# Moving two weight sums in the fifth unit, and block sums, sums of x and the turn of w in the sixth, of a linear-attention and SiLU kernel

## The chip, the cores and the metric

The kernel runs on one core of a Trainium2 chip. A core has five engines that each work through their own instructions in order: TensorE (PE, matrix products; its weight loads are shown apart as PEld), VectorE (DVE), ScalarE (ACT), GpSimd (POOL) and SyncE (SP), which here issues nearly all DMA transfers. They wait for each other through semaphores. SBUF is the on-chip memory of 128 partitions, PSUM holds the results of TensorE. The metric is the time of one execution on the device, in microseconds; lower is better.

## The reference, cut to what matters

First a linear attention with a decaying state (batch 4, 8 heads, 768 time steps, head size 48), then a two-layer block with SiLU on its output (3072 tokens, 384 to 2048 to 384), all in float32:

```python
for t in range(S):
    kt, vt, rt, wt = k[:, :, t], v[:, :, t], r[:, :, t], w[:, :, t]
    cur = einsum('bhd,bhe->bhde', u[None] * kt, vt)
    y[:, :, t] = einsum('bhd,bhde->bhe', rt, state + cur)
    state = wt[..., None] * state + einsum('bhd,bhe->bhde', kt, vt)
x = y.transpose(0, 2, 1, 3).reshape(B * S, H * D)
h = x @ w_in
out = (h / (1 + exp(-h))) @ w_out
```

## The kernel before, in words

The 768 steps are cut into 6 stretches of 128, and the batch into 2 pairs, which gives 12 **units** of 128 steps and two batch rows each. They are numbered from 0, so the fifth unit has `i == 4` (`NPAIR` is 4, `NFAST` is 3) and the sixth `i == 5`. The order of all instructions is written out by hand; there is no scheduler, and each engine follows its own part of the recorded order.

Inside a unit the 128 by 128 scores of a head are built in 7 levels. Level `l` takes blocks of `2 << l` steps: the later half's queries against the earlier half's keys. For that the decays `w` are turned so that time runs along the free dimension (`turn`, a transpose on VectorE, two per unit), and `product` (POOL, L414) multiplies neighbours, from 128 values to 64 and so on, into `tw1` to `tw7`. `grow_keys` (POOL, L646) multiplies the keys on to the next level, and `grow_queries` and `prepare` (VectorE, L628 and L783) the queries. `odd_keys` (ScalarE, L616) copies half of the keys to where the next level reads them. From the fourth unit on the products of two levels come in a `burst` (TensorE, L704): levels 3 and 4, then levels 5 and 6. `keep_level` puts them into `score`, by masked copies on VectorE (L722) for small levels and by copies on ScalarE (L804) for the levels 5 and 6.

The levels 0 to 2, the 8 by 8 blocks along the diagonal, are done another way from the fifth unit on. `block_bonus` (POOL, L497) makes products of queries and keys in token order, in steps 0 to 7, and `block_sum` (VectorE, L534) reduces them into `block_sums`: sum 0 and 1 after steps 1 and 2, sum 2 after step 4, sum 3 after step 6, sum 4 after step 7. Step 4 and step 7 write the same tile `ruk`, so sum 2 has to read it before step 7. `block_move(i, False)` then sends `block_sums` to DRAM (`kept`, L556), and `block_move(i, True)` brings it back in another layout in five transfers (`spare<-kept`, L561 and L563). The tokens of the next unit (`load_rk`, L158) go into tiles that step 7 reads last. `block_turn` (L567) shuffles one half of the block sums, and `block_write` (VectorE, L573) puts them into `score`, once for each half.

Beside a unit's attention runs the two-layer block of earlier units. In each call of `mix(i)` there is a list of groups with a count: the steps of a group are recorded, then so many steps of the block are recorded behind them. These are the seven quarter products of the second layer of unit `i - 2` (`quarter`, L1333, whose partial results are joined on VectorE in L1341 and on ScalarE in L1338) and then the twenty products of the first layer of unit `i - 1` (`first_layer`, L1189). The quarter products add into PSUM places that are used again: the seventh of them waits until VectorE has added the fifth to a known part (`ob`, L1341). The first layer from unit 3 on needs fewer products because sums of parts are formed first, of the weights once and for all (`in_weight_sum`, L1128, named `q1` to `q19`) and of x for every unit (`sums_of_x`, VectorE, steps 0 to 7, L1150 to L1170). Its products stand in the order

```python
ORDER = (20, 18, 14, 13, 2, 15, 4, 7, 19, 16, 1, 12, 9, 11, 3, 6, 10, 5, 8, 17)
```

(the keys alone), and VectorE joins their results in PSUM between them (`join`, L1216). Product 9 reads the weight sum `q9`; product 17 adds to a PSUM place that the join behind product 10 writes. The second burst stands between the products 11 and 3. At the end, `sums` (VectorE, L1304) makes eight differences of the SiLU results, which the quarter products of the next `mix` read from `temps`.

At the end of a unit `end[1]` records the state products, the scores by the values (L847 to L868), the turn of the next unit's keys (L365), two block sums, and the update. The next unit begins with the turn of its queries and `grow_own` (POOL, L655).

## Time and profile before

| what | us |
|---|---|
| median of three runs (568.08 to 572.91) | 568.59 |
| the profiled execution | 568.89 |
| its span, first to last instruction | 567.1 |
| TensorE busy in the span | 555.3 |
| VectorE busy | 477.7 |
| GpSimd busy | 395.4 |
| ScalarE busy | 275.1 |
| sixth unit (212.85 to 257.60): length, TensorE busy | 44.75, 43.17 |
| seventh unit (257.60 to 300.19) | 42.59, 42.59 |
| eighth unit (300.19 to 342.62) | 42.43, 42.43 |

The granted TensorE clock was 1.00 throughout. A line of a timeline has the start, the time taken, the engine, the source line, the operation and its tiles, the shape, and after `x` how many neighbours were merged into the line. In brackets stands how long the engine had been idle before, and which engine and line ended that. `SPq` is SyncE's issuing of a transfer, not the transfer. Matrix products overlap, so a product's time can be longer than its step in the sequence. `p_o`, `p_h`, `p_m`, `p_sc` are PSUM tiles, `tk`, `tr`, `tw` the turned keys, queries and decays.

### The profile page before, as it was taken

The page shows a single profiled execution, that of the slowest core. Times are in us where ns is not written, and L with a number is a line of the kernel's source. Part 1 is how long each engine was busy: PE and PEld are TensorE (multiplying, and loading weights), DVE is VectorE, ACT ScalarE, POOL GpSimd, SP SyncE. Part 2 cuts the span into 40 slices and gives each one's busy share as a digit, 9 for nine tenths or more (in the row PEclk, how much of TensorE's full clock was granted, in tenths as well). Part 3 has the DMA queues.
Part 4 walks back from the last instruction along what each step waited for, and adds up shares of the span by engine and source line. Part 5 has one row for each costly group of instructions (what it writes and reads, how often), then busy time and mean ns, then how long its engine had stood idle before and what let it go on. Part 6 is the DMA issues. An engine that isn't in the chain of part 4 may idle for free.

```text
span 567.1 us, 18885 instructions
## 1 busy us (share of the span) xinstructions
PE 555.3 (98%) x7782; PEld 517.6 (91%) x7782; DVE 477.7 (84%) x744; ACT 275.1 (49%) x620; POOL 395.4 (70%) x447
## 2 busy tenths in 40 slices
PE   8989999999999999999999999999999999999997
PEld 8767786699889989899999999999999999999997
DVE  6969788999999999899989989989989989882250
ACT  5679696362371373374274274274274272371330
POOL 5998998717879998797696696696696696700000
PEclk9999999999999999999999999999999999999999
DMA  9866967345445355365465454455555462102000
GB/s 204 266 139 185 241 210 143 48 60 118 107 73 102 77 109 93 60 130 94 101 103 93 104 100 90 106 96 93 108 92 96 91 108 65 38 5 57 29 9 21
DMA packets 206485, 57.59 MB, mean 102 GB/s; under 512 B 186048, under 2 KB 198208, under 8 KB 206400
## 3 DMA queue, kind: packets, MB, share of 16 engines
q1 hardware_dynamic: 203712, 54.23, 46.2%
q10 hardware_dynamic: 2688, 2.16, 1.5%
q8 instruction: 61, 1.00, 0.8%
q14 instruction: 24, 0.20, 0.1%
HBM read 47.14 MB, written 9.18 MB: 99 GB/s over the span
## 4 chain that ended last, share of the span: by engine, by line
PE 73%; POOL 10%; DVE 6%; SPq 5%; DMA 3%; issue 2%; ACT 0%; ACTq 0%; DVEq 0%; POOLq 0%
PE p_o L1333 23%; PE p_o L1189 14%; PE p_h L1189 9%; PE p_h L1082 7%; PE p_h L1333 4%; PE p_m L1271 4%; SPq L127 3%; PE p_sc L704 2%; PE p_m L868 2%; POOL tk L646 2%; DMA raw<-in_w_dram 2%; PE p_sc L1333 2%; PE p_m L847 1%; PE p_m L704 1%; DMA w_out_sb<-in_moe_w_in_dram 1%
## 5 line engine op out<-in xcount | busy, mean ns | idle before, releaser
L646 POOL TENSOR_TENSOR tk<-tk,tw 128x256 f32<-128x256 f32 x112 | 93.0, 851 | 7.9 <-DVE tw L414 3.8
L1333 PE MATMUL p_o<-own,temps 128*128 128x192 f32 x496 | 82.8, 326 | 0.0
L1333 PEld LDWEIGHTS p_o<-own,temps 128*128 128x128 f32 x496 | 80.8, 190 | 0.2 <-DVE temps L1304 0.2
L1189 PE MATMUL p_o<-xt,w_in_sb 128*64 128x128 f32 x1152 | 72.2, 273 | 0.8 <-POOL w_in_sb L1128 0.8
L414 POOL TENSOR_TENSOR tw<-tw 128x256 f32<-128x256 f32 (+6 forms) x71 | 40.5, 571 | 41.4 <-DVE tw L365 38.0
L1082 PE MATMUL p_h<-xt,w_in_sb 128*128 128x256 f32 x288 | 66.1, 384 | 1.8 <-POOL w_in_sb L260 1.6
L1189 PEld LDWEIGHTS p_o<-xt,w_in_sb 128*64 128x64 f32 x1152 | 64.6, 137 | 1.1 <-POOL w_in_sb L1128 1.1
L1082 PEld LDWEIGHTS p_h<-xt,w_in_sb 128*128 128x128 f32 x288 | 53.6, 190 | 10.0 <-POOL w_in_sb L260 2.4
L1333 PE MATMUL p_o<-w_out_sb,gt 128*128 128x192 f32 x308 | 54.5, 330 | 1.3 <-DVE ob L1341 1.3
L497 POOL TENSOR_TENSOR ruk<-tokens_rk 128x384 f32<-128x384 f32 x48 | 53.1, 1127 | 2.5 <-DMA tokens_rk<-in_k_dram 2.5
L628 DVE TENSOR_TENSOR tr<-tr,tw 128x512 f32<-128x512 f32 x57 | 51.9, 910 | 1.0 <-PE p_m L704 0.4
L1333 PEld LDWEIGHTS p_o<-w_out_sb,gt 128*128 128x128 f32 x308 | 50.0, 190 | 2.4 <-DVE ob L1341 1.6
L655 POOL TENSOR_TENSOR tk<-tk,tw 128x256 f32<-128x256 f32 x32 | 24.7, 800 | 31.6 <-DVE tk L365 31.6
L1304 DVE TENSOR_TENSOR temps<-gt 128x512 f32<-128x512 f32 (+1 forms) x48 | 43.1, 934 | 0.0
L1338 ACT COPY partial<-p_o 128x192 f32<-128x192 f32 x31 | 9.9, 319 | 67.5 <-PE p_o L1333 67.5
L1213 ACT ACTIVATE gt<-p_o 128x512 f32<-128x512 f32 x45 | 26.0, 601 | 25.7 <-PE p_o L1189 25.7
L616 ACT COPY tk<-tk 128x256 f32<-128x256 f32 x52 | 20.9, 402 | 33.7 <-POOL tk L646 25.0
L1333 PE MATMUL p_o<-w_out_sb,temps 128*128 128x192 f32 x176 | 30.4, 326 | 0.0
L722 DVE COPY_PREDICATED score<-mask,p_sc 128x512 f32<-128x512 int8 x38 | 28.4, 806 | 1.4 <-PE p_sc L704 1.3
L1333 PE MATMUL p_h<-w_out_sb,gt 128*128 128x192 f32 x168 | 29.1, 326 | 0.0
L497 POOL TENSOR_TENSOR spare<-tokens_rk 128x384 f32<-128x384 f32 x24 | 28.5, 1200 | 0.6
L1333 PEld LDWEIGHTS p_o<-w_out_sb,temps 128*128 128x128 f32 x176 | 28.9, 190 | 0.0
(251 smaller groups left out, 1316.7 us busy)
## 6 DMA issues: line engine op xcount, KB each, us to landing
w_out_sb<-in_moe_w_in_dram SPq DMA_DIRECT2D x6, 768.0 KB, 7.6
turned<-yt SPq DMA_DIRECT2D x18, 192.0 KB, 2.6
xt<-turned SPq DMA_DIRECT2D x9, 384.0 KB, 3.2
w_out_sb<-in_moe_w_out_dram SPq DMA_DIRECT2D x4, 768.0 KB, 5.2
own<-in_moe_w_out_dram SPq DMA_DIRECT2D x4, 768.0 KB, 5.7
tokens_w<-in_w_dram SPq DMA_DIRECT2D x8, 384.0 KB, 4.4
tokens_rk<-in_r_dram SPq DMA_DIRECT2D x7, 384.0 KB, 4.3
tokens_rk<-in_k_dram SPq DMA_DIRECT2D x7, 384.0 KB, 5.3
```

Source lines behind the costliest of these rows:

```text
L414: engine.tensor_tensor(out=up, in0=t[:, :, 0::2], in1=t[:, :, 1::2], op=ALU.mult)
L497: mul = lambda out, one, two: nc.gpsimd.tensor_tensor(out=out, in0=one, in1=two, op=ALU.mult)
L628: nc.vector.tensor_tensor(out=odd, in0=odd, in1=tw[i][l][:, :, 0::2][:, :, :, None].to_broadcast([128, Q, L >> (l + 1), c]), op=ALU.mult)
L646: nc.gpsimd.tensor_tensor(out=out, in0=have, in1=odd_products(i, l, b, *blocks), op=ALU.mult)
L655: nc.gpsimd.tensor_tensor(out=have, in0=have, in1=odd_products(i, l, b, [2, NP * ni]), op=ALU.mult)
L722: nc.vector.copy_predicated(out=dst, mask=masks[l][:, :, None].to_broadcast([128, NB, NP, ni, c]), data=sc[e].rearrange("p (b q) (i c) -> ...
L1082: nc.tensor.matmul(p_h[:, a, :], lhsT=w_in_sb[:, c, f * 128:(f + 1) * 128], rhs=xt[i][:, c, :], start=(a == 0 and c == 0), stop=(a == 1 an ...
L1189: nc.tensor.matmul(p[h:h + PD, q, :], lhsT=left[:, f:f + PD], rhs=right, start=first and q == 0, stop=q == 3, skip_group_check=True)
L1213: nc.scalar.activation(out=g(f, t), in_=have, func=AF.Silu)
L1271: nc.tensor.matmul(po[i, b], lhsT=gt[i, f // 2][:, f % 2, b * L:(b + 1) * L], rhs=w_out_sb[:, f, :], start=(f == 0), stop=(f == FC - 1))
L1304: nc.vector.tensor_tensor(out=out, in0=one, in1=two, op=op)
L1333: nc.tensor.matmul(p, lhsT=left(f), rhs=right[:, f, :], start=which in (0, 1, 3) and f == 0, stop=f == FH - 1, skip_group_check=True)
```

## The change

In the fifth unit the weight sums q5 and q9 are recorded one group earlier, ahead of `go_on(4, 4)`, which holds the key products of level 4. In the sixth unit (`tight`), sum 2 goes from ahead of `prepare(5, 3)` to behind step 3 of the sums of x, where step 7 of the bonus and steps 4 to 6 of the sums of x follow it, in a group of their own. Sum 4 and the sending of the block sums to DRAM go two groups later, behind the token loads of the next unit and the first four loads of its r, and right ahead of the transfers that bring them back. The two turns of the next w and its seven products, which stood around `keep_level(5, 4)` and `go_on(5, 4)`, go to the end of the unit, between the two block writes. No instruction is added or taken away.

```diff
+                tight = i == NPAIR + 1
-                keys_2 = [(odd_keys, i, 2), (grow_keys, i, 2, False), (grow_queries, i, 2), *sum_steps(i, 2)]
+                keys_2 = [(odd_keys, i, 2), (grow_keys, i, 2, False), (grow_queries, i, 2), *at(not tight, *sum_steps(i, 2))]
...
-                          ([*at(i in (NPAIR + 1, len(units) - 1), (sums_of_x, j, 0, 1)), (sums_of_x, j, 2), *bonus_steps(i, 6, 7), (sums_of_x, j, 3, 4, 5, 6), *loads("k", 3)], 2),
-                          ([(burst, i, 3), *at(i > NPAIR + 1, *sum_steps(i, 3)), (keep_level, i, 3), *at(i == NPAIR + 1, *sum_steps(i, 3)), *sum_steps(i, 4)], 2),
-                          ([(block_move, i, False), *at(ahead, (load_rk, i + 1, (0, 1))), *at(ahead and i > NPAIR + 1, (turn, i + 1, 0, "w"))], 1),
+                          ([*at(tight or i == len(units) - 1, (sums_of_x, j, 0, 1)), (sums_of_x, j, 2), *bonus_steps(i, 6), *at(not tight, *bonus_steps(i, 7)), (sums_of_x, j, 3), *at(not tight, (sums_of_x, j, 4, 5, 6)), *loads("k", 3)], 1 if tight else 2),
+                          *at(tight, ([*sum_steps(i, 2), *bonus_steps(i, 7), (sums_of_x, j, 4, 5, 6)], 1)),
+                          ([(burst, i, 3), *at(not tight, *sum_steps(i, 3)), (keep_level, i, 3), *sum_steps(i, 3 if tight else 4)], 2),
+                          ([*at(not tight, (block_move, i, False)), *at(ahead, (load_rk, i + 1, (0, 1))), *at(ahead and not tight, (turn, i + 1, 0, "w"))], 1),
                           ([*loads("r", 0)], 1),
-                          ([(block_move, i, True), *at(i == NPAIR + 1, (turn, i + 1, 0, "w")), *at(ahead, (turn, i + 1, 1, "w"), *products_of(i + 1, 0, 1, 2)), (keep_level, i, 4)], 2),
-                          ([(go_on, i, 4), *at(ahead, *products_of(i + 1, 3, 4, 5, 6))], 1),
+                          ([*at(tight, *sum_steps(i, 4), (block_move, i, False)), *at(not tight, (block_move, i, True)), *at(ahead and not tight, (turn, i + 1, 1, "w"), *products_of(i + 1, 0, 1, 2)), (keep_level, i, 4)], 2),
+                          ([*at(tight, (block_move, i, True)), (go_on, i, 4), *at(ahead and not tight, *products_of(i + 1, 3, 4, 5, 6))], 1),
...
-                          ([(keep_level, i, 5, 1), (keep_level, i, 6, 1)], 1),
+                          ([(keep_level, i, 5, 1), (keep_level, i, 6, 1), *at(tight, *both(turn, i + 1, "w"), *products_of(i + 1, *range(NL)))], 1),
...
-            for place, engine, names in ((0, nc.gpsimd, ("u1", "u", "q19")), (5, nc.gpsimd, ("q7",)), (8, nc.gpsimd, ("q8", "q1")),
-                                         (9, nc.gpsimd, ("q5", "q9")), (14, nc.gpsimd, ("q6", "q17"))):
+            for place, engine, names in ((0, nc.gpsimd, ("u1", "u", "q19")), (5, nc.gpsimd, ("q7",)), (8, nc.gpsimd, ("q8", "q1", "q5", "q9")),
+                                         (14, nc.gpsimd, ("q6", "q17"))):
```

## The prediction

> **What bounds the kernel.** I read the page first, then TensorE's waits, then the timelines of the fifth and sixth unit, engine by engine. All times below are on the clock of the profiled run of before.
>
> ```profile
> span 567.1 us, 18885 instructions
> PE 555.3 (98%) x7782; PEld 517.6 (91%) x7782; DVE 477.7 (84%) x744; ACT 275.1 (49%) x620; POOL 395.4 (70%) x447
> ```
>
> TensorE works in 555.3 of 567.1 us, and the change takes no matrix product away. So all it can win is idle time of TensorE in two of twelve units. The list of TensorE's waits says how much that is:
>
> ```profile
> PE p_o L1333 <- DVE ob L1341: 1.3, 1, 1.3
> PE p_o L1189 <- POOL w_in_sb L1128: 0.8, 1, 0.8
> PE p_m L704 <- POOL tk L646: 0.2, 1, 0.2
> ```
>
> Each happens once: the 0.83 us at 199.55 in the fifth unit, the 1.35 us at 228.72 and the 0.23 us at 247.3 in the sixth. The table of stretches, one per unit (sixth, then seventh), shows the room: length, then TensorE's busy time, then the other engines'.
>
> ```profile
> 212.85:257.60 44.75, 43.17 (x693) 41.69 (x689) 40.99 (x63) 20.40 (x52) 38.65 (x46) 1.00 0.50 92
> 257.60:300.19 42.59, 42.59 (x693) 41.58 (x689) 39.36 (x60) 20.58 (x52) 33.48 (x38) 1.00 0.53 99
> ```
>
> The sixth unit idles 1.58 us, the seventh not at all, but there VectorE (third figure, 39.36 of 42.59) is nearly as full as TensorE. That is where the bill for moved work would be sent. VectorE's timeline over the border of the two units:
>
> ```profile
> 227.86 1.13 DVE L534 TENSOR_REDUCE block_sums<-ruk 128x4 f32<-128x192 f32 x4 [0.89 <-POOL ruk L497]
> 229.66 0.36 DVE L1341 TENSOR_TENSOR ob<-p_o,partial 128x192 f32<-128x192 f32 x1
> ...
> 248.89 0.22 DVE L567 STREAM_SHUFFLE spare<-spare 128x64 f32<-128x64 f32 x1
> ...
> 261.27 1.30 DVE L365 STREAM_TRANSPOSE tk<-raw 128x512 f32<-128x512 f32 x2
> ...
> 272.88 0.36 DVE L1341 TENSOR_TENSOR ob<-p_o,partial 128x192 f32<-128x192 f32 x1
> ```
>
> From 248.26 to 280.2 the timeline shows no idle time of VectorE. The last line is the seventh unit's `ob` addition, for which TensorE's last quarter product (L1333) waits: it ends at 273.24 and that product starts at 273.30. So there is 0.06 us of slack, and whatever delays VectorE in that stretch delays TensorE by the same amount.
>
> **The change, part by part.**
>
> *Fifth unit, POOL.* Before, POOL runs the level-4 key products (196.02, 1.67 us), then q5 and q9 (197.65 and 199.00, to 200.34), then the level-5 key products (1.65, to 201.94). Now q5 and q9 come first and end at 198.7, so product 9 no longer waits: 0.83 us gone. The level-4 keys end at 200.35 and the level-5 keys at 202.0, as POOL's total is the same. The burst that needs them would start at 201.46 (202.29 less 0.83), its second half at 201.97: a tie. Nothing else on POOL moves. Of the 0.83, what goes on depends on VectorE, which carries the chain from there: ScalarE's silu for product 9 can move only from 201.53 to 201.25, its next copy from 202.41 to 201.75, so VectorE's next join from 203.03 to 202.4. I take **-0.6** (bounds 0 and -0.83).
>
> *Sixth unit, the 1.35 us.* The four reductions (1.13, after 0.89 waiting for POOL) leave the place ahead of L783 and `ob`. VectorE's query product ends at 226.96, L783 takes 0.72, `ob` then runs from 227.6 to 228.0, before TensorE is ready at 228.72. The reductions now stand behind the first sums of x, end near 232, and POOL's product that overwrites their input starts at 235.72: covered by 3.7 us. The two turns of w (1.2 us at 239.2) leave, sum 4 goes behind the next join, and the level-5 keys no longer stand behind w products. So the 0.23 goes too, and with 0.1 of slack in a join TensorE comes to the last part of the unit **1.67** us earlier. This gain lasts only if VectorE can follow.
>
> *Sixth unit, the block sums' way through DRAM.* SyncE's queue before:
>
> ```profile
> 238.71 0.33 SPq L556 DMA_DIRECT2D kept<-block_sums  x1
> 239.13 0.56 SPq L158 DMA_DIRECT2D tokens_rk<-in_r_dram  x1
> 239.74 0.59 SPq L158 DMA_DIRECT2D tokens_rk<-in_k_dram  x1
> 240.38 2.06 SPq L127 DMA_DIRECT2D raw<-in_r_dram  x4
> 242.54 0.41 SPq L561 DMA_DIRECT2D spare<-kept  x1
> 242.99 3.81 SPq L563 DMA_DIRECT2D spare<-kept  x4
> ```
>
> Now `kept` stands behind the two token loads (384 KB each) and four loads of r, with its return right behind it. The token loads wait for POOL's last product that reads the old tokens, which ends at 237.70 (235.72 and 1.98). So they issue at 237.8, and `kept` 3.4 us later (242.54 less 239.13), at 241.2. A transfer in that place took 4.1 us to land (the longest of the five `spare` transfers; the last took 1.8), so 245.3. In the fifth unit five issues straight after each other began over 2.5 us. The last is out at 247.9 and lands 1.8 later: **249.8** (bounds: 247.2, when VectorE wants it, and 251.3, if a write needs 1.4 more). Before, it was there at 248.2 and the shuffle ran at 248.89. The queue's later loads move back by 1.3 us and stay ahead of the yt copy that the following transfer awaits.
>
> [...]
>
> *End of the sixth unit.* Both turns of w (1.25 us) now stand behind the first block write, ahead of the join for product 17. With the shuffle at 249.8: block write 1.5, turns 1.25, join 0.65, together with the shuffle's 0.25 to 253.5. TensorE wants product 17 at 250.9 (252.53 less 1.67) and waits 2.6: it is 1.0 later than before. POOL gets seven w products (2.69 and 1.59 = 4.28 us) after the turns, and three bonus products (3.47, 1.44, 1.34) behind them, so it works until about 263.3, where before it was free from 258.27:
>
> ```profile
> 262.06 3.06 POOL L655 TENSOR_TENSOR tk<-tk,tw 128x256 f32<-128x256 f32 x4 [3.78 <-DVE tk L365]
> ```
>
> VectorE's eight subtractions (L1304) stand there. While POOL works one takes 1.48 us, while it rests 0.68; before they took 8.2 us in all, half of them slow. Starting at 255.4, I get five slow ones and three fast ones: 9.05, so 0.85 more (bounds 5.4 and 11.1 in all). [...]
>
> *The sum.* The seventh unit's `ob` moves by 249.8 - 248.9 = 0.9 for the shuffle, 1.25 for the turns and 0.85 for the subtractions: 3.0 later, and TensorE with it, since its slack was 0.06. The 1.67 is eaten inside these 3.0. With the fifth unit: 3.0 - 0.6 = **+2.4 us**. The profiled execution took 568.89 around its span of 567.1, so 571.3; the median of the runs is 568.59, 0.3 below that execution, so the sum may read high by that.
>
> **Rivals.**
>
> *The block sums are back in time.* If `kept` lands in 1.5 us, as the first one before did with nothing ahead of it, and its return is not held either, the shuffle runs when wanted, at 247.2. Then `ob` moves by -1.7 + 1.25 + 0.85 = 0.4, and the sum is -0.2: 568.7. For it: `kept` is a write, the loads ahead are reads of DRAM. Against it: the 4.1 us of `spare` in that very place. [...]
>
> *Faster: POOL leaves VectorE its pace.* POOL's idle time now lies between its last key product and the turns, and six of the seven w products are short (0.2 to 0.9 us). If the eight subtractions find it quiet, they take 5.4 instead of 8.2. The sum is then -0.6 + 0.9 + 1.25 - 2.8 = -1.3: 567.6. It decides from five fast subtractions of eight. Against it: the bonus products, 6.25 us of long operations, follow without a break.
>
> *Much slower.* If the block sums land after 253 us, the scores are late too, and the sum passes +5.7: 574.6 or more. Only the fifth unit's 5.5 us landings, taken twice, get there.
>
> *The edit does not do what it says.* If the burst waits for the later level-4 and level-5 keys, the 0.83 us only changes its name and the sum is +3.0: 571.9.
>
> **How the numbers follow.** The forecast (569.9 to 573.2, likeliest 571.3) gets 0.55, the block sums in time 0.20, the faster one 0.17, the empty edit 0.03, the much slower one 0.05. The range 567.0 to 573.4 takes in the second, most of the third, and the landing bounds (247.2 and 251.3 are -2.6 and +1.5 around 249.8). One per cent is 5.7 us, about what a measurement of this kernel can tell from no change; all cases but one lie inside: faster 0.01, same 0.95, slower 0.04.
>
> **What would show it.** In the profile after, the two waits of 0.8 and 1.3 us are gone from TensorE's list. In their place stands a wait of product 17, a `first_layer` product, for VectorE at the end of the sixth unit, about 2.6 us, and one of the last quarter product for `ob` in the seventh, about 2. The shuffle has an idle time ended by a DMA. If the shuffle follows without idle time, the DMA step is wrong; if the seventh unit's `ob` comes before TensorE wants it, the VectorE step is wrong. The prediction fails at the top if the late w products also hold the key products of the seventh unit, which had 5.3 us of cover (the level-3 keys end at 270.83, the burst starts at 276.09).

## The result and the profile after

The changed kernel takes 572.68 us (median of nine executions, 570.24 to 575.36) against 568.59 for the kernel before (568.08 to 572.91, also nine). The ratio is 1.0063, with a 95% interval of 1.0036 to 1.0091: a loss of about 0.6%, inside the one per cent that the prediction called no change. The ratio is taken over all the executions and is not the quotient of the medians, which would be 1.0072. A single execution is left out of a ratio as slow, one of 577.33 us of the kernel with the fifth unit's part alone, 1.7% above the fastest of that kernel. The profiled execution took 570.24 us around a span of 568.4; that of before took 568.89 around 567.1. So the profiled pair differs by 1.35 us and the medians by 4.1. Both figures need an explanation, and they have different ones. (The profiled execution of before lies 0.3 above its median, that of after 2.4 below.)

The changed kernel has two lines more around L1030, so all later line numbers shift by two: L1218 is the join of L1216, L1306 the differences of L1304, L1335 the quarter product, L1343 the `ob` addition, L1191 the first layer. First the page of after, its span and engines:

```profile
span 568.4 us, 18883 instructions
PE 555.5 (98%) x7782; PEld 517.4 (91%) x7782; DVE 476.6 (84%) x744; ACT 274.8 (48%) x620; POOL 395.7 (70%) x447
```

TensorE's work is what it was (555.5 against 555.3), so the difference is idle time. TensorE's waits of after: total, times, longest.

```profile
PE p_o L1191 <- DVE p_o L1218: 2.8, 1, 2.8
...
PE p_o L1335 <- DVE ob L1343: 0.3, 1, 0.3
PE p_h L1191 <- DVE p_h L1218: 0.2, 1, 0.2
```

The waits of 0.8 (for a weight sum) and 1.3 (for `ob` in the sixth unit) are gone, and so is the 0.2 for the key products. In their place stands one wait of 2.8 us, of a first-layer product for a join. The timelines of TensorE and of VectorE say which one and why:

```profile
253.58 1.09 PE L1191 MATMUL p_o<-xt,w_in_sb 128*64 128x128 f32 x16 [2.82 <-DVE p_o L1218]
```

```profile
250.17 0.01 DVE L567 LOAD_MASK_SELECT spare<-spare  x1 [2.75 <-DMA spare<-kept]
250.19 0.23 DVE L567 STREAM_SHUFFLE spare<-spare 128x64 f32<-128x64 f32 x1
250.46 1.30 DVE L573 COPY_PREDICATED score<-late_masks,spare 128x1024 f32<-128x1024 int8 x1
251.65 1.29 DVE L365 STREAM_TRANSPOSE tw<-raw 128x512 f32<-128x512 f32 x2
252.86 0.67 DVE L1218 TENSOR_TENSOR p_o<-gt,p_h 128x512 f32<-128x512 f32 x1
253.44 1.81 DVE L573 COPY_PREDICATED score<-late_masks,spare 128x1024 f32<-128x1024 int8 x1
255.14 1.89 DVE L1306 TENSOR_TENSOR temps<-gt 128x512 f32<-128x512 f32 x2
...
262.49 1.29 DVE L365 STREAM_TRANSPOSE tk<-raw 128x512 f32<-128x512 f32 x2
...
274.21 0.36 DVE L1343 TENSOR_TENSOR ob<-p_o,partial 128x192 f32<-128x192 f32 x1
```

It is product 17. VectorE, which before had nothing to wait for here, stands still for 2.75 us until the block sums are back from DRAM, then does the shuffle, one block write and both turns of w, and only then the join that product 17 needs. The chain that ended last, from 236 us on, runs through the same transfers (start, time taken, what):

```profile
241.28 4.06 DMA kept<-block_sums
245.35 0.39 SPq L561
...
247.40 2.65 DMA spare<-kept
...
250.19 0.24 DVE spare L567
```

The write `kept`, behind two token loads and four loads of r, took 4.06 us to land, and the last of the five return transfers 2.65.

Where the profiled 1.3 us lie is seen best from the lengths of the units, each measured from one state update (the products in L913, in both kernels) to the next. The sixth unit begins with these lines of TensorE's timeline, before and then after:

```profile
212.04 0.53 PE L913 MATMUL p_sc<-vt,kq 128*48 128x48 f32 x16
```

```profile
211.56 0.53 PE L913 MATMUL p_sc<-vt,kq 128*48 128x48 f32 x16
```

The fifth unit begins at times up to 1.3 us apart in the profiled executions, although the kernels are alike up to there, so spans alone would blur effects of this size.

| kernel | fifth | sixth | seventh | sum |
|---|---|---|---|---|
| before | 46.26 | 44.74 | 42.53 | 133.53 |
| after | 45.76 | 46.32 | 42.76 | 134.84 |

The eighth to tenth unit take 42.43 us and the rest behind them 140.5 in both, so +1.31 us is the whole of it.

### The profile page after: what moved, and what is told of

Same layout as the page of the kernel before. It is cut to its first block, busy times and chain, and to the rows that moved or that the text cites. A ratio compares the mean times of both kernels' runs of the same rounds, so it can differ in the third digit from the quotient of the medians.

```text
span 568.4 us, 18883 instructions
## 1 busy us (share of the span) xinstructions
PE 555.5 (98%) x7782; PEld 517.4 (91%) x7782; DVE 476.6 (84%) x744; ACT 274.8 (48%) x620; POOL 395.7 (70%) x447
## 4 chain that ended last, share of the span: by engine, by line
PE 81%; DVE 7%; ACT 3%; DMA 3%; SPq 2%; POOL 2%; issue 2%; DVEq 0%; POOLq 0%; ACTq 0%
PE p_o L1335 24%; PE p_o L1191 15%; PE p_h L1191 10%; PE p_h L1084 8%; PE p_h L1335 4%; PE p_m L1273 4%; PE p_sc L704 3%; PE p_m L868 2%; PE p_sc L1335 2%; PE p_m L847 2%; DVE tr L628 2%; SPq L127 2%; PE p_m L704 2%; DVE score L722 1%; PE p_sc L823 1%
## 5 line engine op out<-in xcount | busy, mean ns | idle before, releaser
L1335 PE MATMUL p_o<-own,temps 128*128 128x192 f32 x496 | 82.8, 326 | 0.0
L1335 PEld LDWEIGHTS p_o<-own,temps 128*128 128x128 f32 x496 | 80.8, 190 | 0.2
L1191 PE MATMUL p_o<-xt,w_in_sb 128*64 128x128 f32 x1152 | 72.3, 273 | 2.8 <-DVE p_o L1218 2.8
L414 POOL TENSOR_TENSOR tw<-tw 128x256 f32<-128x256 f32 (+6 forms) x71 | 42.4, 597 | 42.5 <-DVE tw L365 39.1
L1191 PEld LDWEIGHTS p_o<-xt,w_in_sb 128*64 128x64 f32 x1152 | 64.7, 137 | 3.1 <-DVE p_o L1218 3.1
L1335 PE MATMUL p_o<-w_out_sb,gt 128*128 128x192 f32 x308 | 54.5, 330 | 0.3 <-DVE ob L1343 0.3
L1335 PEld LDWEIGHTS p_o<-w_out_sb,gt 128*128 128x128 f32 x308 | 50.0, 190 | 1.5 <-DVE ob L1343 0.9
L1306 DVE TENSOR_TENSOR temps<-gt 128x512 f32<-128x512 f32 (+1 forms) x48 | 42.0, 913 | 0.0
L1335 PE MATMUL p_o<-w_out_sb,temps 128*128 128x192 f32 x176 | 30.5, 327 | 0.1
L1335 PEld LDWEIGHTS p_o<-w_out_sb,temps 128*128 128x128 f32 x176 | 28.8, 190 | 0.3 <-ACT partial L1340 0.3
L1335 PE MATMUL p_h<-w_out_sb,gt 128*128 128x192 f32 x168 | 29.1, 326 | 0.0
```

The source lines that it names most:

```text
L414: engine.tensor_tensor(out=up, in0=t[:, :, 0::2], in1=t[:, :, 1::2], op=ALU.mult)
L1191: nc.tensor.matmul(p[h:h + PD, q, :], lhsT=left[:, f:f + PD], rhs=right, start=first and q == 0, stop=q == 3, skip_group_check=True)
L1306: nc.vector.tensor_tensor(out=out, in0=one, in1=two, op=op)
L1335: nc.tensor.matmul(p, lhsT=left(f), rhs=right[:, f, :], start=which in (0, 1, 3) and f == 0, stop=f == FH - 1, skip_group_check=True)
```

## Experiments

Two theories were to be tested, with two rivals. **A:** the block sums' late return stalls VectorE, and VectorE's lateness costs TensorE wherever it shows. **B:** TensorE's idle time of 2 to 3 us makes its granted clock drop to half for a while in many executions, which explains why the median lies 2.4 us above the profiled execution. The rivals: the late turns of w cost by themselves, and a drift of the chip. Each table row gives the median of the executions and the ratio to the kernel before on the same chip with its interval; the units are from the profiled execution, and a star marks a unit in whose records the granted clock fell.

| kernel | us | ratio [95%] | fifth, sixth, seventh | sum |
|---|---|---|---|---|
| fifth unit only | 568.34 | 1.0001 [0.9992, 1.0010] | 45.98, 45.02, 42.54 | 133.54 |
| sixth unit only | 572.73 | 1.0079 [1.0060, 1.0097] | 46.24, 47.64*, 42.43 | 136.31 |
| sums sent ahead of the loads | 568.18 | 1.0014 [0.9996, 1.0032] | 45.75, 44.64, 42.77 | 133.16 |
| turns of w back | 570.28 | 1.0040 [1.0025, 1.0056] | 45.74, 48.48*, 42.43 | 136.65 |
| filler for TensorE | 570.24 | 1.0027 [1.0012, 1.0042] | 45.82, 46.49, 42.75 | 135.06 |
| sums back later still | 572.19 | 1.0066 [1.0039, 1.0093] | 45.85, 48.25*, 42.43 | 136.53 |
| join ahead of block writes | 571.16 | 1.0044 [1.0028, 1.0060] | 46.17, 43.50, 47.39* | 137.06 |
| sent ahead, turns back, writes behind the join | 569.29 | 1.0007 [0.9993, 1.0022] | 45.99, 45.71, 42.43 | 134.13 |
| sent and brought back ahead of the loads | 569.23 | 1.0023 [1.0004, 1.0041] | 45.73, 43.33, 44.82 | 133.88 |
| sent ahead, turns back | 568.06 | 0.9993 [0.9985, 1.0002] | 45.75, 44.82, 42.55 | 133.12 |
| sent and brought back ahead, turns back | 568.59 | 1.0006 [0.9996, 1.0016] | 46.28, 44.50, 42.97 | 133.75 |

The fifth unit takes 45.73 to 46.28 us in the kernels that have the new places of q5 and q9, although nothing else differs there. Differences of half a microsecond in the sum are therefore not argued from. A unit with a star holds up to 1.7 us (half of 3.41) that the fallen clock cost. Only one execution of each kernel has a trace; of the others there are the time and the mean granted clock.

### The fifth unit's part alone

On the kernel before:

```diff
-            for place, engine, names in (..., (8, nc.gpsimd, ("q8", "q1")),
-                                         (9, nc.gpsimd, ("q5", "q9")), ...):
+            for place, engine, names in (..., (8, nc.gpsimd, ("q8", "q1", "q5", "q9")),
...
```

> The kernel before with only q5 and q9 moved ahead of the level-4 key products in the fifth unit. All theories: product 9's wait of 0.83 us is gone from TensorE's list, the next unit begins about 0.5 us earlier (0.48 in the profile after), and the sixth unit's wait for ob stays at 1.3 us or grows by what was gained, since VectorE sets it: span 566.5 to 567.1, time 0 to 0.6 us under the kernel before. If the fifth unit's part were the harmful one: over 568.

Measured: 568.34 us, ratio 1.0001, so not under the kernel before. The wait for `q9` is gone and the fifth unit is 0.28 shorter, but TensorE's waits of this kernel show who takes it:

```profile
PE p_o L1333 <- DVE ob L1341: 1.5, 1, 1.5
```

The wait for `ob` at the start of the sixth unit was 1.35 us before and is 1.51 now, and the sixth unit is 0.28 longer, as much as the fifth had won. Counted from the start of the fifth unit, the product behind that wait starts at 64.30 us here (229.99 less 165.69) and in the kernel before (230.07 less 165.77). TensorE comes earlier to a wait that ends when VectorE says so.

### The sixth unit's part alone

On the changed kernel:

```diff
-            for place, engine, names in (..., (8, nc.gpsimd, ("q8", "q1", "q5", "q9")),
+            for place, engine, names in (..., (8, nc.gpsimd, ("q8", "q1")),
+                                         (9, nc.gpsimd, ("q5", "q9")), ...):
```

> The changed kernel with the fifth unit as before. Theory A (the block sums' late return stalls product 17): the whole loss is here, product 17 waits 2.7 to 3.0 us, span 568.7 to 569.2. Theory B (TensorE idle for nearly 3 us lowers its granted clock in many executions, which is why the median of the changed kernel, 572.7, lies 2.4 us over its profiled execution): the repeated runs show a granted clock of 0.991 to 0.997 and scatter by some us, while the kernel before beside it shows 1.000. Rival to B (a drift of the chip): both kernels scatter alike.

Measured: 572.73 us, ratio 1.0079. All of the loss belongs to the sixth unit's part. This profiled execution also shows what that of after does not. First its waits, then its table of stretches of 2 us, in which the last three figures are the granted clock (1.00 is full), the busy share of the DMA engines and what they moved in GB/s:

```profile
PE p_o L1191 <- DVE p_o L1218: 3.0, 1, 3.0
```

```profile
252.00:254.00 2.00, 1.30 (x24) 1.13 (x26) 2.00 (x3) 1.96 (x5) 1.78 (x2) 1.00 0.85 162
254.00:256.00 2.00, 2.00 (x50) 1.94 (x50) 2.00 (x3) 1.58 (x4) 1.84 (x3) 0.64 0.45 64
256.00:258.00 2.00, 2.00 (x38) 1.83 (x32) 1.90 (x4) 0.00 (x0) 1.76 (x4) 0.50 0.28 36
258.00:260.00 2.00, 2.00 (x54) 1.95 (x51) 2.00 (x3) 1.85 (x4) 2.00 (x3) 1.00 0.21 29
```

The wait ended at about 252.7. From 254.58 to 257.99, for 3.41 us, TensorE ran at half its clock. In the profile of after the same stretch, behind a wait of 2.82 us, stays at 1.00:

```profile
254.00:256.00 2.00, 2.00 (x58) 1.77 (x56) 2.00 (x2) 2.00 (x6) 1.84 (x3) 1.00 0.53 85
256.00:258.00 2.00, 2.00 (x68) 1.92 (x60) 1.90 (x4) 1.03 (x3) 1.76 (x4) 1.00 0.41 55
```

One such drop lowers the mean clock of an execution by 0.003 (half of 3.41 us in 568); the profiled executions with one have 0.997, those with two 0.994. The executions of after have mean clocks of 1.000 (570.24 us), 0.997 (571.52 and 571.61), 0.994 (570.75, 572.68, 572.73, 572.76, 575.36) and 0.991 (574.82). Four of the traces, this one among them, also have a drop near the start, between 39.3 and 43.3 us. It costs nothing that can be seen: the fifth unit, up to which the kernels are alike, begins at 164.50 us with it (sent and brought back ahead, turns back) and at 164.82 and 165.77 without (sent and brought back ahead; before). The expectation of a clock of 1.000 for the kernel before was missed: 11 of its 26 executions beside these runs have a mean of 0.996 or 0.997, and they took 567.55 to 568.27 us, the others 567.95 to 569.43. These executions have no trace, so that theirs is the early drop is likely and not shown. One mean of 0.997 does not tell of a drop in the sixth unit.

### The block sums sent ahead of the loads

On the changed kernel; the turns stay late.

```diff
-                          ([*at(not tight, (block_move, i, False)), *at(ahead, (load_rk, i + 1, (0, 1))), ...], 1),
-                          ([*loads("r", 0)], 1),
-                          ([*at(tight, *sum_steps(i, 4), (block_move, i, False)), ...], 2),
+                          ([*at(not tight, (block_move, i, False)), *at(ahead and not tight, (load_rk, i + 1, (0, 1))), ...], 1),
+                          ([*at(not tight, *loads("r", 0))], 1),
+                          ([*at(tight, *sum_steps(i, 4), (block_move, i, False), (load_rk, i + 1, (0, 1)), *loads("r", 0)), ...], 2),
```

> The changed kernel with one difference in the sixth unit: the block sums are sent to DRAM ahead of the two token loads and the four loads of r, not behind them; the turns of w stay late. Theory A: kept issues at 238.9, its return lands near 248.2 instead of 250.0, product 17 waits about 0.9 us instead of 2.8, span 566.2 to 567.0, and by theory B the granted clock is 1.000 in most runs, so the median is 567.9 to 568.8. Rival (the late turns and w products are what costs, through VectorE and POOL at the border of the units): span 568.0 or more, and ob in the seventh unit still near 274.2.

Measured: 568.18 us, ratio 1.0014; the span of 565.8 lies even a little under the expected 566.2 to 567.0. The sixth unit falls from 46.32 to 44.64. The order of `kept` and six loads in SyncE's queue was nearly all of the loss. VectorE's timeline and TensorE's wait of this kernel:

```profile
247.46 0.01 DVE L567 LOAD_MASK_SELECT spare<-spare  x1 [0.65 <-DMA spare<-kept]
```

```profile
PE p_o L1191 <- DVE p_o L1218: 1.0, 1, 1.0
```

VectorE's wait falls from 2.75 to 0.65 and product 17's from 2.8 to 1.0. The 1.0 that is left is about the late turns (1.29 us ahead of the join); in the last kernel below, which has the turns back as well, product 17 does not wait. Two of eleven executions took 572.5, with mean clocks of 0.997 and 0.991. They have no trace, and the kernel before has such executions too (one of nine, one of 32), so that the 1.0 us of idle time made them is not shown.

### The turns of w back, the sums still late

On the changed kernel:

```diff
-                          ([*at(tight, *sum_steps(i, 4), (block_move, i, False)), ..., *at(ahead and not tight, (turn, i + 1, 1, "w"), *products_of(i + 1, 0, 1, 2)), (keep_level, i, 4)], 2),
-                          ([*at(tight, (block_move, i, True)), (go_on, i, 4), *at(ahead and not tight, *products_of(i + 1, 3, 4, 5, 6))], 1),
+                          ([*at(tight, *sum_steps(i, 4), (block_move, i, False)), ..., *at(tight, (turn, i + 1, 0, "w")), *at(ahead, (turn, i + 1, 1, "w"), *products_of(i + 1, 0, 1, 2)), (keep_level, i, 4)], 2),
+                          ([*at(tight, (block_move, i, True)), (go_on, i, 4), *at(ahead, *products_of(i + 1, 3, 4, 5, 6))], 1),
...
-                          ([(keep_level, i, 5, 1), (keep_level, i, 6, 1), *at(tight, *both(turn, i + 1, "w"), *products_of(i + 1, *range(NL)))], 1),
+                          ([(keep_level, i, 5, 1), (keep_level, i, 6, 1)], 1),
```

> The changed kernel with the two turns of w and the seven w products back at the places before, between the sums and the level-4 scores; the block sums still leave behind the loads. Theory A: the shuffle still waits for the return, near 250, product 17 waits about 1.4 us, one more wait of about 0.6 us for a join in mid unit, span 567.3 to 568.3. Rival (turns and products cost): product 17's wait is gone, span 566.0 to 566.8.

Measured: 570.28 us, ratio 1.0040. With the turns out of the way product 17 still waits 1.98 us, as the shuffle still comes late, at 250.92 behind 2.82 us of waiting. So the late turns are a part of the loss and not the cause of it. (The wait was expected at 1.4.) The five executions with a mean clock of 0.999 or 1.000 took 568.96 to 570.28 us, against 570.24 of the one such execution of after. In this profiled execution the clock fell to half from 255.34 to 258.76, again for 3.41 us, behind an idle time of 1.98 us.

### Filler for TensorE

On the changed kernel, in `first_layer`. The kernel makes 18 transposes of the identity, into a PSUM place whose content nobody needs, right ahead of product 17:

```diff
+        if (i, n) == (NPAIR, 17):
+            room = made[NPAIR + 1, 6][0].rearrange("p q t -> p (q t)")[:, 0:L]
+            for x in range(18):
+                nc.tensor.transpose(room, ident, ident)
```

> The changed kernel with 18 idle matrix products (128x128 transposes of the identity into a PSUM place that is free by then, about 2.0 us in all) put ahead of product 17 in the sixth unit, inside its wait of 2.8 us. Nothing that VectorE or the transfers wait for moves. Theory B (the idle stretch lowers the granted clock): less than 1 us of idle time is left, so the granted clock stays at 1.000 there, and the median falls from 572.7 to 570.0 to 571.0, with little scatter. Rival (the clock drops for another reason): median 572 or more as in the changed kernel.

This tells A's loss from B's: the join is as late as before, only TensorE's idle time is shorter. TensorE's timeline of this kernel (its line numbers are higher by four more: L1195 is the first layer, L1222 the join):

```profile
250.51 2.18 PE L1189 MATMUL p_m<-ident 128*128 128x128 f32 x18
253.57 1.10 PE L1195 MATMUL p_o<-xt,w_in_sb 128*64 128x128 f32 x16 [0.87 <-DVE p_o L1222]
```

Product 17 starts at 253.57, where it started in after (253.58), and the three units sum to 135.06, 0.2 more than in after. Yet the median is 570.24 us, ratio 1.0027 against 1.0063, and the eleven executions lie within 569.41 to 571.43, with mean clocks of 0.996 to 1.000, where eight of the nine of after have 0.991 to 0.997. The median is that of the one execution of after without a drop. The kernel of the next section, with a wait of 3.1 us and no filler, ran beside these on the same chip and scatters from 570.21 to 576.43. Useless work in the same wait took about 2 us off (0.0036 of 568; the intervals of the two ratios touch, at 1.0036 to 1.0042). B is shown in kind: this part of the loss goes with TensorE's idle time and not with the lateness of the join, and so does the granted clock, whose lowest mean is 0.996 with 0.87 us of idle time there and 0.991 with 2.82. Whether the clock explains all of the 2 us is left open below. A drift of the chip is ruled out, as the kernel before ran beside these without such a scatter (567.6 to 569.1 in 31 of 32 executions).

### The sums back later still

On the changed kernel, the loads of the next unit's w tokens and four further loads of r go ahead of the return:

```diff
-                          ([*at(tight, (block_move, i, True)), (go_on, i, 4), ...], 1),
-                          ([*at(ahead, (load_rk, i + 1, (2,)))], 1),
-                          ([*loads("r", 1)], 1),
+                          ([*at(tight, (load_rk, i + 1, (2,)), *loads("r", 1), (block_move, i, True)), (go_on, i, 4), ...], 1),
+                          ([*at(ahead and not tight, (load_rk, i + 1, (2,)))], 1),
+                          ([*at(not tight, *loads("r", 1))], 1),
```

> The changed kernel with the next unit's w tokens and four more loads of r put ahead of the return of the block sums, so that these land later still, near 252. Theory A: product 17 waits 4 to 5 us, span 570 to 571 without any loss of clock. Theory B: every run now has its granted clock at 0.994 or lower, median 573 to 577. Rival to A (the turns set the end): no more than 0.3 us over the changed kernel.

Measured: 572.19 us, ratio 1.0066, and product 17 waits 3.13 us: a miss, as the wait hardly grew. The five added issues (3.9 us together) fell into the 4 us in which SyncE stands waiting for `kept` to land. Issue slots ahead of that landing were free here. What counts is the landing itself: 4.06 us after the issue behind six loads (after), 1.5 us with none ahead (the kernel with the sums brought back at once). So the edit did not make the sums much later: on the sixth unit's own clock the shuffle comes 0.35 us later than in after, and the wait is 0.31 longer. That fits A, but it does not reach past the 0.3 that was allowed to the rival. B's forecast for this kernel was missed in part: three of the nine executions have a mean clock of 1.000 and took 570.21 to 570.97 us, and the median lies below the 573 to 577 expected. The other six have 0.991 to 0.997 and took 571.00 to 576.43.

### The join ahead of the block writes

On the changed kernel, the shuffle, the block write and the turns go behind the join that product 17 needs:

```diff
-                          ([(burst, i, 5), ..., (go_on, i, 6), (block_turn, i), (block_write, i, 1)], 2),
-                          ([(keep_level, i, 5, 1), (keep_level, i, 6, 1), *at(tight, *both(turn, i + 1, "w"), *products_of(i + 1, *range(NL)))], 1),
-                          ([(block_write, i, 0)], 1),
+                          ([(burst, i, 5), ..., (go_on, i, 6), *at(not tight, (block_turn, i), (block_write, i, 1))], 2),
+                          ([(keep_level, i, 5, 1), (keep_level, i, 6, 1)], 1),
+                          ([*at(tight, (block_turn, i), (block_write, i, 1)), (block_write, i, 0), *at(tight, *both(turn, i + 1, "w"), *products_of(i + 1, *range(NL)))], 1),
```

> The changed kernel with the shuffle, both block writes, the turns and the w products put behind the join for product 17, so that this product no longer waits for the block sums. Theory A in full (VectorE's lateness is what costs, wherever it shows): product 17's wait is gone, but VectorE still begins its eight subtractions near 254.5, so the wait moves to the seventh unit's ob, 2.0 to 2.8 us, and the span stays at 568.0 to 569.0. Simple reading (the wait at product 17 is the loss): span 565.5 to 566.3.

Measured: 571.16 us, ratio 1.0044. Product 17's wait is gone and the sixth unit is down to 43.50 us, 1.24 less than before the change. TensorE's timeline of the seventh unit shows the bill:

```profile
274.46 4.55 PE L1335 MATMUL p_o<-w_out_sb,gt 128*128 128x192 f32 x16 [3.01 <-DVE ob L1343]
```

The same lateness of VectorE stands one unit on, at `ob`, and right behind it the clock fell to half from 275.08 to 278.50 (the product group takes 4.55 us instead of 2.87). The four executions with a mean clock of 1.000 took 569.97 to 570.70 us, as much as that of after (570.24). This is A: the wait was put in another place and not made shorter. The span of 568.0 to 569.0 was missed (570.0), by the drop and by a wait of 3.01 instead of 2.0 to 2.8.

### Three orders with the return in time

Three kernels look for an order that keeps the gains. The first is the kernel that sends the sums ahead of the loads, with the turns back as well and the shuffle and block writes behind the join:

```diff
+                          ([*at(tight, *sum_steps(i, 4), (block_move, i, False), (load_rk, i + 1, (0, 1)), *loads("r", 0)), ..., *at(tight, (turn, i + 1, 0, "w")), *at(ahead, (turn, i + 1, 1, "w"), *products_of(i + 1, 0, 1, 2)), (keep_level, i, 4)], 2),
...
+                          ([*at(tight, (block_turn, i), (block_write, i, 1)), (block_write, i, 0)], 1),
```

> A version meant to beat both: the fifth unit and sums 2 and 4 as changed, the block sums sent ahead of the loads, the turns and w products at the places before, shuffle and block writes behind the join for product 17. Theory A: product 17 does not wait, ob in the seventh unit waits at most 0.5 us, a join in mid unit costs about 0.5 us; the fifth to seventh unit take 132.5 to 133.0 us together, against 133.5 in the kernel before and 134.8 in the changed one; time 0.5 to 1.0 us under the kernel before. Theory B: no loss of clock, as no idle stretch is over 1 us. If VectorE's order matters in some other way, over 133.5.

Measured: 569.29 us, ratio 1.0007, with 134.13 us for the three units. It missed: the shuffle comes at 250.97, and now the products of the scores and the values wait 0.88 us for a block write. All eleven executions have a mean clock of 0.999 or 1.000, as B had it. The second brings the sums back at once and loads behind, with the turns late as in the changed kernel:

```diff
+                          ([*at(tight, *sum_steps(i, 4), (block_move, i, False), (block_move, i, True), (load_rk, i + 1, (0, 1)), *loads("r", 0)), ..., (keep_level, i, 4)], 2),
...
+                          ([(burst, i, 5), ..., *at(ahead and not tight, *bonus_steps(i + 1, 0)), (go_on, i, 6), *at(tight, *bonus_steps(i + 1, 0)), (block_turn, i), (block_write, i, 1)], 2),
```

> The changed kernel with the block sums sent and brought back at once, and the token loads and four loads of r behind both; the product that reads the new tokens goes behind the last key products on POOL. Theory A: the return lands near 245, before VectorE wants it at 247.4, product 17 waits less than 0.2 us, VectorE begins its subtractions about 2.5 us earlier than in the changed kernel, and the fifth to seventh unit take 132.0 to 132.8 us together (133.5 before, 134.8 changed, 133.2 with the sums only sent first). Theory B: no loss of clock. Time 0.7 to 1.5 us under the kernel before. If the late turns still hold VectorE: ob in the seventh unit waits over 1 us and the three units take 133.3 or more.

Measured: 569.23 us, ratio 1.0023. With nothing ahead of it `kept` landed in 1.5 us (issued at 237.88, the return issued at 239.42) and the shuffle ran without a wait at 246.13. The sixth unit took 43.33 us, 1.4 less than before, and the seventh gave back 2.3 of it, in TensorE's timeline:

```profile
272.68 2.87 PE L1335 MATMUL p_o<-w_out_sb,gt 128*128 128x192 f32 x16 [2.12 <-DVE ob L1343]
```

VectorE had no idle time between the shuffle and this addition; from one to the end of the other it took 26.50 us, against 24.35 before. The turns are 1.2 of the 2.1 more. So it is the second case of the expectation (a wait over 1 us, 133.3 or more), and B's "no loss of clock" did not hold for all executions: two of twelve have mean clocks of 0.994 (570.41 us) and 0.991 (574.49). The same kernel with the turns and their products back tells whether the late token loads are the rest:

```diff
-                          ([*at(tight, *sum_steps(i, 4), (block_move, i, False), (block_move, i, True), (load_rk, i + 1, (0, 1)), *loads("r", 0)), ..., (keep_level, i, 4)], 2),
+                          ([*at(tight, *sum_steps(i, 4), (block_move, i, False), (block_move, i, True), (load_rk, i + 1, (0, 1)), *loads("r", 0)), ..., *at(tight, (turn, i + 1, 0, "w")), *at(ahead, (turn, i + 1, 1, "w"), *products_of(i + 1, 0, 1, 2)), (keep_level, i, 4)], 2),
```

> The kernel with the block sums sent and brought back ahead of the loads, and now the two turns of w and its products back in their places of before as well. With the turns late, the sixth unit had shrunk to 43.33 us (before: 44.74) and the seventh had grown to 44.82 (42.53), with a wait of 2.1 us for ob. If VectorE's own work behind the shuffle made that wait (1.29 us of turns, and subtractions slowed by the w products of GpSimd beside them), it falls to 0.8 us or less, the sixth unit grows by up to 0.9, the three units sum to 133.0 to 133.4 against 133.5, and the time is 568.0 to 568.5. If the late token loads made it, because the next unit's bonus products start late on GpSimd and run beside the subtractions, the wait stays near 2 us, the sum is 134 or more and the time 569 to 570. No drop of the granted clock is expected in the first case, as no idle of TensorE reaches 2 us.

Measured: 568.59 us, ratio 1.0006. The wait for `ob` fell to 0.27 us and VectorE's stretch to 24.60, with the token loads still behind the return. That is the first case of the expectation: VectorE's own work, with GpSimd's w products beside it. The token loads can have a small part in it, as GpSimd's products that need them began at 248.36 here and at 249.31 there. The sixth unit grew by 1.17, a little more than the 0.9 expected, and the time lies 0.1 us above the range given. The sum of 133.75 misses 133.0 to 133.4; the fifth unit alone took 0.5 us more in this execution than in most, with no wait on record that explains it. The turns and the w products came back together, so their shares are not told apart.

The last kernel undoes both moves: the sums sent ahead of the loads, the turns back. What is left of the change is the fifth unit and the places of sum 2, sum 4 and the sums of x.

```diff
+                          ([*at(tight, *sum_steps(i, 4), (block_move, i, False), (load_rk, i + 1, (0, 1)), *loads("r", 0)), ..., *at(tight, (turn, i + 1, 0, "w")), *at(ahead, (turn, i + 1, 1, "w"), *products_of(i + 1, 0, 1, 2)), (keep_level, i, 4)], 2),
+                          ([*at(tight, (block_move, i, True)), (go_on, i, 4), *at(ahead, *products_of(i + 1, 3, 4, 5, 6))], 1),
...
+                          ([(keep_level, i, 5, 1), (keep_level, i, 6, 1)], 1),
```

> The changed kernel with the block sums sent ahead of the loads and the turns and w products at the places before, so what is left of the change is the fifth unit, sum 2 and sum 4. If the late turns cost by themselves, this is better than the version with the sums sent first and the turns late: the three units under 133.1 us, ob in the seventh unit without a wait. If they cost nothing, or pay, because the joins in mid unit come earlier: 133.2 us or more, with about 0.5 us of wait for a join in mid unit.

Measured: 568.06 us (567.21 to 568.37), ratio 0.9993 with 0.9985 to 1.0002. It is the best of the eleven and not measurably better than the kernel before. The sum of 133.12 falls between the two cases of the expectation, and it is that of the kernel with the sums sent first and the turns late (133.16): once the sums are back in time, no price of the late turns is seen. Both early waits are gone here, and the sixth and seventh unit still sum to 87.37 us against 87.27.

## Why the prediction was right, and where it was not

The forecast was 571.3 us, within 567.0 to 573.4 and most likely no change by more than one per cent. The median is 572.68 and the ratio 1.0063, so the time lies in the range and the change is below one per cent. The mechanism was the predicted one in the main: the block sums come back late, and product 17 waits for them through VectorE. But the sum of +2.4 us stands between a profiled +1.3 and a median of +4.1, so it is near the median partly by luck: terms that were too small, one that was too large and one that was missing offset each other. Term by term, the units counted from their own starts (sixth unit at 212.04 before, 211.56 after):

| term of the sum | predicted | measured |
|---|---|---|
| fifth unit | -0.6 | -0.48 |
| shuffle later | +0.9 | +1.78 |
| shuffle, writes and join, without the turns | 0 | -0.47 |
| turns of w in that place | +1.25 | +1.21 |
| eight subtractions | +0.85 | -0.82 |
| from there to `ob` | 0 | +0.11 |
| sum, at the seventh unit's `ob` | +2.4 | +1.33 |
| from the profiled execution to the median (clock, and what is open below) | not foreseen | about +2.4 |

The four terms between the shuffle and the sum add up to 0.03, where +2.1 was forecast: from the shuffle to the end of the `ob` addition VectorE took 24.38 us, against 24.35 before, although the turns were added there. So nearly the whole of the profiled loss is that the block sums came 1.78 later, less what the fifth unit won.

*Fifth unit.* Right: -0.48 in the trace (but the fifth unit scatters by half a microsecond between traces of the same order), and a new wait of 0.21 for a join takes most of the rest of the 0.83, as the passage on VectorE's chain said. Alone it gains nothing, since the wait for `ob` swallowed it. The sixth unit's part had to take that wait away first.

*The block sums' way.* Right in kind, and the size is within its bounds. `kept` landed 4.06 us after its issue (predicted 4.1), the return's last issue ended at 247.85 (predicted 247.9). On the sixth unit's own clock the shuffle is 0.9 later than forecast, mainly because the token loads wait for GpSimd's last product, which ended at 237.84. The working had it at 237.70 on a clock on which the whole unit starts 0.48 later, which makes 0.6 of the 0.9. The last transfer took 2.65 instead of 1.8. Both are counted from the start of its issue; the working set the 1.8 behind the end of the issue, and that hid about half of the difference. The rival "back in time" was not met, but its price can be read from the two kernels that send `kept` first and have the turns late: the shuffle ran at 247.5 (behind 0.65 of waiting) and at 246.1 (forecast for that case: 247.2), and the times are 568.2 and 569.2 us (forecast: 568.7). `kept` itself landed 4.06 us after its issue behind the loads (after) and 1.5 us after it without them (sent and brought back ahead).

*End of the sixth unit.* Product 17 was forecast at 253.5 with a wait of 2.6; it started at 253.58 with 2.82. That it hangs on the return and on the order is shown by the kernels that send the sums ahead (1.0) and that put the join first (none).

*The subtractions.* This is the step that failed. "Five slow ones and three fast ones: 9.05" stands against 7.35 us (255.14 to 262.49; before, 253.10 to 261.27, which is 8.17). By the 1.48 and 0.68 printed beside it the sum would even be 9.44. The working let GpSimd keep its pace and VectorE lose. VectorE's first two subtractions of before took 2.89 us, against 1.89 after, and GpSimd's w products of before stood elsewhere:

```profile
253.10 2.89 DVE L1304 TENSOR_TENSOR temps<-gt 128x512 f32<-128x512 f32 x2
```

```profile
240.57 2.69 POOL L414 TENSOR_TENSOR tw<-tw 128x512 f32<-128x512 f32 x3 [2.87 <-DVE tw L365]
244.71 1.59 POOL L414 TENSOR_TENSOR tw<-tw 128x64 f32<-128x64 f32 x4
```

GpSimd's timeline of after:

```profile
253.02 6.20 POOL L414 TENSOR_TENSOR tw<-tw 128x512 f32<-128x512 f32 x7 [5.12 <-DVE tw L365]
```

Seven products that took 4.28 us before, in their old places, took 6.20 here, so in this stretch GpSimd lost 1.92 us. The first block write, too, ran at 1.30 us instead of 1.86, at a time when GpSimd rested for 5.12 us. Beside the w products VectorE's first six subtractions took 0.68 to 1.09 us each, and only the last two, which run beside the bonus products, 1.48 and 1.37. The kernel with the turns back shows the other side: there GpSimd is idle from 256.00 to 261.78, seven of the eight subtractions take 0.68 to 0.69 us, and all eight take 6.0. That VectorE's gain in after comes from GpSimd's loss is read from timelines and not tested apart. The 7.35 lies about half way between the forecast and the 5.4 of the "faster" rival, without GpSimd being quiet, which was that rival's reason.

*The seventh unit's `ob`.* Forecast as a wait of about 2 us, measured 0.26: it follows from the subtractions, as VectorE was only 1.33 us later and TensorE itself was late by product 17.

*What was not foreseen.* The clock. No term of the sum is for a drop of it behind idle time (with the join first a product group took 4.55 us instead of 2.87 there). Whether a wait of 2.8 us costs 2.8 us or more could not be read from the profile of before, where the longest wait of TensorE in these units was 1.35 us and the clock stood at 1.00.

## What to carry to other kernels

A small write whose result is awaited goes ahead of large loads in its queue, not behind them: here that order alone was worth 1.7 us of the three units, and 2.8 us by the two ratios. Where two engines are both full, a wait taken from one place can come back at the next place where they meet (here the 2.82 us at product 17 as 3.01 at `ob` with the join first, and as 2.12 with the sums brought back ahead), so the sum of unit lengths, not the list of waits, tells what was won. And where a trace shows idle time of TensorE like the 2.82 us here, in the middle of dense work, one profiled execution is not enough (570.24 us here, against a median of 572.68): look at the granted clock of several executions before a time is taken from it.

## What the hardware showed beside that

Behind idle times of 1.98 us (turns back) and of 3.0 to 3.1 us (sixth unit only, sums later still, join first) the traces show drops of the granted clock to 0.5, each for 3.41 us. The profiled execution of after had 2.82 us and no drop, while six of its other executions have mean clocks of 0.991 to 0.994, which make room for two drops or three, the early one included. In the profiled executions with a drop the three units sum to 136.3 to 137.1, against 134.8 in that of after without, 1.5 to 2.2 us more by kernels that differ in other parts too. Mean clocks below 0.995 stand in six of nine executions of after, in two of nine with 1.98 us (turns back) and in two of twelve with 2.12 us (sent and brought back ahead); with 1.0 (sums sent ahead) two of eleven took over 572 us, with the filler (0.87) none of eleven stands out. Long executions are not tied to a long wait alone: the kernel before (1.35) has two over 572 us among its 107 executions, and the one of 577.33 us, with a mean clock of 0.982, is of the kernel with the fifth unit's part alone, whose longest wait in these units is 1.5.

The traces also show where the drops began. In the two that have an early and a late one, the beginnings lie whole multiples of 3.413 us apart: 39.54 and 254.58 us with the sixth unit only (63 times 3.413), 39.56 and 275.08 with the join first (69 times). The record of the clock begins at 7.03 us and changes at 566.82 in before (164 times), and in after it begins at 6.79 and changes at 569.99 (165 times); both changes lie behind TensorE's last product. So the idle time is counted here in windows of 3.413 us that end or begin at such a change. In the window just ahead of the four drops in the sixth and seventh unit TensorE was idle for 1.53 (sixth unit only), 1.55 (sums later still), 1.87 (turns back) and 2.79 us (join first). In after, windows counted back from the change of the clock at 569.99 us, behind the last instruction, part the wait in two, at 252.55: 1.79 us of idle time in the window ahead and 1.03 in the next, and neither brought a drop.

A wait that such windows cut in one way or another would explain why the same kernel has a drop in one execution and none in the next; with one trace of each kernel this is the author's estimate and not shown. How much idle time in a window brings a drop is not shown either: none came behind 1.79 us in after, nor behind 1.50 with the sixth unit only, one window earlier, while one came behind 1.53. Open is also the rest of the scatter. One drop of 3.41 us at half clock can cost 1.7 us at most by its length (the product group with the join first took 4.55 us instead of 2.87), but the median of after lies 2.4 over its profiled execution, and its execution of 575.36 us lies 5.1 over it, with a mean clock that makes room for two drops.
